# Attention and MLP kernel on one core: when weights and V are queued, over which queues the first loads go, and whether k or q is prepared first

## The chip, the cores and the metric

The kernel runs on one core of a Trainium2 chip. The time is device microseconds of that core. Three executions of the kernel before took 317.15, 321.90 and 322.06 us. A run is called "slow" when it is over 1.5% above the fastest of the same kernel, and "fast" otherwise.

A "span" is the length of one profiled execution from its first to its last instruction; it is some 2 us shorter than the time. The engines are TensorE (PE, weight loads PEld), VectorE (DVE), ScalarE (ACT), GpSimd (POOL) and SyncE (SP).

## The reference

Four batches, eight heads, 768 positions, 64 columns per head. Each query attends to the three best of twelve key blocks (by the mean key of the block) and to its own block, causally; then a token-mixing and a channel-mixing MLP run on the result.

```
k_rep = k.reshape(B, H, 12, 64, D).mean(axis=3)
gate  = einsum('bhsd,bhnd->bhsn', q, k_rep)          # causal blocks only
mask  = top 3 blocks of gate, and the own block; causal
x     = softmax(q k^T / 8, masked) v                  # heads side by side: (4, 768, 512)
u     = x + (relu(x^T w_tok1) w_tok2)^T
out   = u + relu(u w_ch1) w_ch2
```

## The kernel before

Two heads make a "pair"; there are 16 pairs, four to a batch. Each pair is prepared in four stages, all of them on chains that cross engines:

- `trq`: six float32 transposes of q on TensorE, a copy to SBUF on ScalarE, two casts on GpSimd.
- `trk`: the same for k, and on VectorE the block sums of k, put into `ks2`.
- `gate`: twelve small float32 matmuls (24 columns each) of q with `ks2`; top 3 on VectorE; result in `bn16`.
- `mask`: six transposes of `bn16`, two copies into the rows that extend q.

Then come scores, exponential (ScalarE), diagonal mask (VectorE) and the product with V (`av`). In the views below `tq` and `tk` are the transposes of q and k, `gps` the gate, `bps` the mask's transposes, `sps` the scores, `aps` the product with V; `qt`, `kt`, `kst` and `ks` are the copies of q and k, the block sums and `ks2`. The MLP work of a batch is strewn between the next batch's pairs, so pairs 0 to 3 have no MLP work beside them.

```python
    def load(i):                                   # q, k on SyncE's queue; V on GpSimd's (it casts to float16)
        ...
        for t, src in ((q32, q), (k32, k)):
            for g in range(2):
                nc.sync.dma_start(out=t[:, :, 64 * g:64 * g + 64], in_=src[b, h + g]...)
        for g in range(2):
            nc.gpsimd.dma_start(out=V16[r][:, g, :, 0:64], in_=v[b, h + g]...)
    ...
        def trk():
            ...
            nc.vector.tensor_reduce(out=kst, in_=kt.rearrange("p (n w) -> p n w", w=64), axis=AX.X, op=ALU.add)
            nc.vector.tensor_copy(out=ks2[r][64:128, 0:NB], in_=kst[64:128, :])
            nc.vector.tensor_copy(out=ks2[r][0:64, NB:2 * NB], in_=kst[0:64, :])
            nc.gpsimd.tensor_copy(out=KA[r][0][0:64, :], in_=kt[0:64, :])
            nc.gpsimd.tensor_copy(out=KA[r][1][64:128, :], in_=kt[64:128, :])
    ...
    preps[0]["trq"](); preps[0]["trk"](); preps[0]["gate"]()
    preps[1]["trq"](); preps[0]["mask"](); preps[1]["trk"]()
    load(2)
    wth = weight_loads()                           # ten pieces of 384 KB, on GpSimd's queue
    for i in range(NP):
        ...
        order = [scores(i, 0, 0)] + stage("gate", i + 1)
        order += [last_av] if last_av else []
        order += [scores(i, 0, 1)] + stage("trq", i + 2) + [scores(i, 0, 2), scores(i, 1, 0)]
        order += stage("mask", i + 1) + [av(i, 0), scores(i, 1, 1)] + stage("trk", i + 2)
        if i + 3 < NP:
            order.append(lambda: load(i + 3))
        if i < 3:
            take, wth = wth[:4], wth[4:]           # weights: no wait in front of the first six
            order += take
        order.append(scores(i, 1, 2))
        last_av = av(i, 1)
```

The order in the program is not quite the order on an engine: a scheduler places the instructions. In the kernel before it put V of pair 0, six weight pieces and V of pair 1 at the head of GpSimd's stream.

The softmax here doesn't subtract the row's maximum and nothing guards it: scores larger than these inputs give would overflow.

Of the kernel before, what the change touches and what calls it, by code (L numbers as in the profile page):

```python
# [9 lines left out]
FP = mybir.dt.float32  # L10
F16 = mybir.dt.float16
AF = mybir.ActivationFunctionType
ALU = mybir.AluOpType
# [13 lines left out]
def kernel(  # L27
# [11 lines left out]
    nc = tc.nc  # L39
    B, H, S, D = q.shape  # L40
    NB = S // 64
# [12 lines left out]
    def const(name, a, dt, eng):  # L54
        t = sp.tile(list(a.shape), dt, tag=name, name=name)
        eng.dma_start(out=t, in_=nc.inline_tensor(a, name=name + "c").ap())
        return t
# [7 lines left out]
    pairs = [(b, h) for b in range(B) for h in range(0, H, 2)]  # L65
    NP = len(pairs)

    loads = {}

    def load(i):  # L70
        b, h = pairs[i]
        q32 = sp.tile([128, NJ, 128], FP, tag="q32", bufs=3, name=f"q32_{i}")
        k32 = sp.tile([128, NJ, 128], FP, tag="k32", bufs=3, name=f"k32_{i}")
        for t, src in ((q32, q), (k32, k)):
            for g in range(2):
                nc.sync.dma_start(out=t[:, :, 64 * g:64 * g + 64],
                                  in_=src[b, h + g].rearrange("(j p) d -> p j d", p=128))
        r = i % (R + 1)
        for g in range(2):
            nc.gpsimd.dma_start(out=V16[r][:, g, :, 0:64],  # L80
                                in_=v[b, h + g].rearrange("(j p) d -> p j d", p=128))
        loads[i] = (q32, k32)

    R = 3
    V16 = [sp.tile([128, 2, NJ, 65], F16, tag=f"V{r}", name=f"V{r}") for r in range(R + 1)]
# [2 lines left out]
    ks2 = [sp.tile([128, 2 * NB], FP, tag=f"ks{r}", name=f"ks{r}") for r in range(R)]  # L88
    bn16 = [sp.tile([128, NJ, 2, 64], F16, tag=f"bn{r}", name=f"bn{r}") for r in range(R)]

    load(0)
    ident32 = const("id32", np.eye(128, dtype=np.float32), FP, nc.scalar)
    for r in range(R):
        nc.vector.memset(ks2[r], 0.0)
        nc.vector.memset(bn16[r], 0.0)
        nc.vector.memset(QA[r][0][64:128, :], 0.0)
        nc.vector.memset(QA[r][1][0:64, :], 0.0)
    for r in range(R + 1):
        nc.vector.memset(V16[r][:, :, :, 64:65], 1.0)
    pidx = np.arange(128)  # L100
    nidx = np.arange(NB)
    jidx = np.arange(NJ)
# [9 lines left out]
    ind64 = np.zeros((64, S), np.float16)  # L112
    ind64[0:NB] = ind_np
    ind_dram = nc.inline_tensor(ind64, name="indc").ap()
    for r in range(R):
        for x in range(2):
            lo = 64 if x == 0 else 0
            nc.sync.dma_start(out=KA[r][x][lo:lo + 64, :], in_=ind_dram)
        if r == 0:
            load(1)  # L120

    w1_16 = sp.tile([128, NJ, DT], F16, tag="w1", name="w1")
    w2_16 = sp.tile([128, 2, S], F16, tag="w2", name="w2")
# [3 lines left out]
    def weight_loads():  # L127
        w1 = moe_w_tok1.rearrange("(j p) t -> p j t", p=128)
        w2 = moe_w_tok2.rearrange("(g p) s -> p g s", p=128)
        c1 = moe_w_ch1.rearrange("(c p) f -> p c f", p=128)  # L130
        c2 = moe_w_ch2.rearrange("(g p) c -> p g c", p=128)
        th = [lambda: nc.gpsimd.dma_start(out=w1_16, in_=w1), lambda: nc.gpsimd.dma_start(out=w2_16, in_=w2)]
        th += [lambda c=c: nc.gpsimd.dma_start(out=wc1_16[:, c, :], in_=c1[:, c, :]) for c in range(NCC)]
        th += [lambda f=f: nc.gpsimd.dma_start(out=wc2_16[:, f:f + 3, :], in_=c2[:, f:f + 3, :])
               for f in range(0, NFC, 3)]
        return th
# [3 lines left out]
    def prep(i):  # L140
        r = i % R
        st = {}

        def trq():
            q32 = loads[i][0]
            ps = big("tq")
            for j in range(NJ):
                nc.tensor.transpose(out=ps[:, 128 * j:128 * j + 128], in_=q32[:, j, :], identity=ident32)  # L148
            qt = sp.tile([128, S], FP, tag="qt", bufs=2, name=f"qt_{i}")
            nc.scalar.copy(out=qt, in_=ps[:, 0:S])  # L150
            st["qt"] = qt
            nc.gpsimd.tensor_copy(out=QA[r][0][0:64, :], in_=qt[0:64, :])
            nc.gpsimd.tensor_copy(out=QA[r][1][64:128, :], in_=qt[64:128, :])

        def trk():
            k32 = loads[i][1]
            ps = big("tk")
            for j in range(NJ):
                nc.tensor.transpose(out=ps[:, 128 * j:128 * j + 128], in_=k32[:, j, :], identity=ident32)  # L159
            kt = sp.tile([128, S], FP, tag="kt", bufs=2, name=f"kt_{i}")  # L160
            nc.scalar.copy(out=kt, in_=ps[:, 0:S])  # L161
            kst = sp.tile([128, NB], FP, tag="kst", bufs=2, name=f"kst_{i}")
            nc.vector.tensor_reduce(out=kst, in_=kt.rearrange("p (n w) -> p n w", w=64),
                                    axis=AX.X, op=ALU.add)
            nc.vector.tensor_copy(out=ks2[r][64:128, 0:NB], in_=kst[64:128, :])
            nc.vector.tensor_copy(out=ks2[r][0:64, NB:2 * NB], in_=kst[0:64, :])
            nc.gpsimd.tensor_copy(out=KA[r][0][0:64, :], in_=kt[0:64, :])
            nc.gpsimd.tensor_copy(out=KA[r][1][64:128, :], in_=kt[64:128, :])

        def gate():  # L170
            gps = bank([128, NJ, 2 * NB], "gps")
            for j in range(NJ):
                nc.tensor.matmul(out=gps[:, j, :], lhsT=st["qt"][:, 128 * j:128 * j + 128],  # L173
                                 rhs=ks2[r], start=True, stop=True)
            gm = sp.tile([128, NJ, 2 * NB], FP, tag="gm", bufs=2, name=f"gm_{i}")
            m8 = sp.tile([128, NJ, 2, 8], FP, tag="m8", bufs=2, name=f"m8_{i}")
            lt = sp.tile([128, NJ, 2 * NB], FP, tag="lt", bufs=2, name=f"lt_{i}")
            nc.vector.tensor_tensor(out=gm, in0=gps, in1=gbias, op=ALU.add)
            for j in range(NJ):
                for x in range(2):  # L180
                    nc.vector.max(out=m8[:, j, x, :], in_=gm[:, j, NB * x:NB * x + NB])
            nc.vector.tensor_tensor(
                out=lt.rearrange("p j (x n) -> p j x n", n=NB),
                in0=gm.rearrange("p j (x n) -> p j x n", n=NB),
                in1=m8[:, :, :, 2:3].broadcast_to([128, NJ, 2, NB]), op=ALU.is_lt)
            nc.vector.scalar_tensor_tensor(out=lt, in0=lt, scalar=MASKV, in1=own, op0=ALU.mult, op1=ALU.max)
            nc.vector.tensor_copy(out=bn16[r][:, :, :, 0:NB], in_=lt.rearrange("p j (x n) -> p j x n", n=NB))

        def mask():
            bps = bank([128, S], "bps", F16)  # L190
            for j in range(NJ):
                nc.tensor.transpose(out=bps[:, 128 * j:128 * j + 128],  # L192
                                    in_=bn16[r][:, j, :, :].rearrange("p x n -> p (x n)"), identity=ident16)
            nc.vector.tensor_copy(out=QA[r][0][64:64 + NB, :], in_=bps[64:64 + NB, :])  # L194
            nc.vector.tensor_copy(out=QA[r][1][0:NB, :], in_=bps[0:NB, :])

        return dict(trq=trq, trk=trk, gate=gate, mask=mask)

    E = {}

# [44 lines left out]
    def mlp(b):  # L245
# [65 lines left out]
        return th  # L311

    preps = [prep(i) for i in range(NP)]
    preps[0]["trq"]()
    preps[0]["trk"]()
    preps[0]["gate"]()
    preps[1]["trq"]()
    preps[0]["mask"]()
    preps[1]["trk"]()
    load(2)  # L320
    wth = weight_loads()
    pend = []
    last_av = None
    for i in range(NP):
        b, h = pairs[i]

        def stage(name, n):
            return [preps[n][name]] if n < NP else []

        order = [scores(i, 0, 0)] + stage("gate", i + 1)  # L330
        order += [last_av] if last_av else []
        first = len(order)
        order += [scores(i, 0, 1)] + stage("trq", i + 2) + [scores(i, 0, 2), scores(i, 1, 0)]
        order += stage("mask", i + 1) + [av(i, 0), scores(i, 1, 1)] + stage("trk", i + 2)
        if i + 3 < NP:
            order.append(lambda: load(i + 3))
        if i < 3:
            take, wth = wth[:4], wth[4:]
            order += take
        order.append(scores(i, 1, 2))  # L340
        last_av = av(i, 1)

        share = sum(c for c, _ in pend) / (4 - i % 4)
        done = 0.0
        for n, f in enumerate(order):
            f()
            want = share * (n + 1 - first) / (len(order) - first)
            while n >= first and pend and done + pend[0][0] / 2 <= want:
                c, g = pend.pop(0)
                g()  # L350
                done += c
        if i % 4 == 3:
            for _, g in pend:
                g()
            if i == NP - 1:
                last_av()
            pend = mlp(b)
# [32 lines left out]
```

## Time and profile before

| what | before |
|---|---|
| span of the profiled execution | 316.6 us |
| TensorE busy | 280.0 us (88%) |
| first score matmul | 28.76 us |
| one of the pairs 1 to 3, from first exponential to first exponential | 10.8, 10.6, 10.5 us |

The page divides the span into 40 slices. Each digit of the row PE is the busy share of TensorE in tenths, of PEclk the granted clock (the share of its full clock that TensorE is given), of DMA the busy share of the transfer engines. From the kernel before:

```profile
PE   1325888888999999999999999999999999899994
...
PEclk9999598778899999999999999999999999999999
...
DMA  9999999675444445646324444330000011100022
```

A slice is 7.9 us. In the first four TensorE has little to do while the transfer engines are full; in the next six it is 80% busy at a lowered clock; after that it is nearly full. So there are three stretches with three limits.

What TensorE waited for up to 42 us (the waits view, its four longest; total us, times, longest):

```profile
PE tq L148 <- DMA q_1_119<-in_q_dram: 6.2, 1, 6.2
PE tq L148 <- DMA q_0_83<-in_q_dram: 5.9, 1, 5.9
PE gps L173 <- DVE ks_77 L166: 3.0, 1, 3.0
PE tk L159 <- DMA k_0_84<-in_k_dram: 2.5, 1, 2.5
```

And the transfers issued up to 28 us (KB each, median us from issue to landing):

```profile
wc_133<-in_moe_w_ch_dram POOLq DMA_DIRECT2D x4, 384.0 KB, 13.6
...
w_131<-in_moe_w_tok_dram POOLq DMA_DIRECT2D x1, 384.0 KB, 8.4
w_132<-in_moe_w_tok_dram POOLq DMA_DIRECT2D x1, 384.0 KB, 10.0
q_1_119<-in_q_dram SPq DMA_DIRECT2D x2, 192.0 KB, 15.8
k_1_120<-in_k_dram SPq DMA_DIRECT2D x2, 192.0 KB, 18.1
```

q and k of pair 1 took 16 and 18 us to land, in the company of six weight pieces that nothing needs before 81 us. On TensorE (its timeline; start us, us, engine, line, operation, out<-in, count; in brackets the idle time before it) the gate of pair 0 comes early and the first scores late:

```profile
14.44 2.73 PE L173 MATMUL gps<-ks_77,qt_142 128*128 128x24 f32 x12 [2.96 <-DVE ks_77 L166]
...
28.76 1.69 PE L212 MATMUL sps<-Q_65,K_71 128*128 128x512 f16 x6
```

The chain of work that ended last shows both limits (start us, us, what):

```profile
8.39 18.29 DMA k_1_120<-in_k_dram
...
52.09 0.80 ACT kt_506 L161
52.91 0.95 DVE kst_508 L163
54.10 0.68 DVE ks_77 L165
...
55.02 1.52 PE gps L173 x12
```

One transfer is 18.3 us of the chain; and in each of the pairs 1 to 3 the copy of k, the block sums, `ks` and the gate follow each other. TensorE's waits between 42 and 82 us say the same:

```profile
PE gps L173 <- DVE ks_79 L166: 1.2, 2, 0.6
PE gps L173 <- DVE ks_78 L166: 0.6, 1, 0.6
PE gps L173 <- DVE ks_77 L166: 0.6, 1, 0.6
```

A wait on the list is short; the chain behind it (copy, sums, `ks`) is longer, because TensorE runs out of other work late. The last reading is the clock, microsecond by microsecond (the prediction says "second" and means this; stretch, us, then busy us and count of PE, PEld, DVE, ACT, POOL; granted clock; DMA share; GB/s):

```profile
54.00:55.00 1.00, 0.42 (x5) 0.18 (x4) 0.95 (x4) 1.00 (x2) 0.75 (x1) 1.00 1.14 206
...
56.00:57.00 1.00, 1.00 (x19) 1.00 (x19) 0.39 (x2) 0.00 (x0) 0.00 (x0) 0.95 0.74 150
57.00:58.00 1.00, 1.00 (x7) 0.94 (x6) 1.00 (x14) 0.00 (x0) 0.78 (x1) 0.50 0.22 36
```

Some 3.4 us at half clock follow in this place, and again at 47, 67 and 77 us. I call them half-clock windows. (The 5 in the row PEclk is a longer one in pair 0, from 33.0 to 39.8 us.)

### The profile page before, as it was taken

What the parts mean: (1) busy time and instruction counts of PE and PEld (TensorE: products, weight loads), DVE (VectorE), ACT (ScalarE), POOL (GpSimd) and SP (SyncE); (2) the same over time, 40 slices, a digit from 0 to 9 for tenths busy, and PEclk for the clock granted to TensorE, in tenths of its full rate; (3) what the DMA queues carried; (4) which work ended last, traced back from release to release, by engine and by line L of the source; (5) the groups of instructions that cost most, each with busy time, mean ns of one, the idle gap of its engine ahead of it and who ended that gap; (6) DMA issues with size and microseconds to landing.
All of it is one profiled execution on the core that took longest, in us unless ns stands there. A gap on an engine that the chain in (4) does not pass through costs nothing.

```text
span 316.6 us, 5878 instructions
## 1 busy us (share of the span) xinstructions
PE 280.0 (88%) x2272; PEld 182.0 (57%) x2272; DVE 181.9 (57%) x624; ACT 141.4 (45%) x185; POOL 86.6 (27%) x110
## 2 busy tenths in 40 slices
PE   1325888888999999999999999999999999899994
PEld 1324665667557675656676766566766655456541
DVE  4223478667496666565975657576865644373321
ACT  2104268556465573526556644354666443214200
POOL 7606565444233333333222324140222000000000
PEclk9999598778899999999999999999999999999999
DMA  9999999675444445646324444330000011100022
GB/s 162 213 191 220 195 215 213 100 104 87 65 62 64 62 64 95 131 100 127 52 36 59 70 90 90 81 79 2 0 2 1 2 66 69 65 2 0 0 101 99
DMA packets 83179, 27.23 MB, mean 86 GB/s; under 512 B 76112, under 2 KB 79568, under 8 KB 83152
## 3 DMA queue, kind: packets, MB, share of 16 engines
q1 hardware_dynamic: 54112, 19.47, 26.5%
q0 software_dynamic: 28320, 7.08, 22.6%
q10 hardware_dynamic: 720, 0.31, 0.4%
q8 instruction: 18, 0.29, 0.4%
q14 instruction: 9, 0.07, 0.1%
HBM read 27.64 MB, written 6.29 MB: 107 GB/s over the span
## 4 chain that ended last, share of the span: by engine, by line
PE 76%; DVE 8%; DMA 7%; ACT 5%; issue 1%; ACTq 0%; SPq 0%
PE sps L212 10%; PE gps L173 7%; PE aps L233 6%; DMA k_1_120<-in_k_dram 6%; PE tq L148 3%; PE ups L267 3%; PE tk L159 3%; PE bps L192 2%; DMA id_113<-id16c 2%; DVE u_3626 L269 1%; PE utps L276 1%; PE c_3376 L299 1%; PE c_3925 L299 1%; PE c_3584 L299 1%; PE c_3485 L299 1%
## 5 line engine op out<-in xcount | busy, mean ns | idle before, releaser
L286 PEld LDWEIGHTS <-wc_133 128*128 128x128 f16 x384 | 37.1, 98 | 26.2 <-issue 0.8
L80 POOL DMA_DIRECT2D V_61<-in_v_dram x8 | 6.8, 847 | 23.7 <-PE aps L233 13.2
L212 PE MATMUL sps<-Q_65,K_71 128*128 128x512 f16 (+3 forms) x48 | 11.6, 330 | 0.7 <-ACT e_12_0_2820 L217 0.5
L299 PEld LDWEIGHTS <-h_3_3628 128*128 128x128 f16 x72 | 7.0, 97 | 8.3
L80 POOL DMA_DIRECT2D V_62<-in_v_dram x8 | 6.6, 828 | 18.6 <-PE aps L233 9.2
L80 POOL DMA_DIRECT2D V_64<-in_v_dram x8 | 6.6, 824 | 18.4 <-PE aps L233 11.5
L212 PE MATMUL sps<-Q_66,K_72 128*128 128x512 f16 (+3 forms) x48 | 10.6, 333 | 0.9 <-ACT e_3_1_820 L217 0.5
L299 PEld LDWEIGHTS <-h_2_2826 128*128 128x128 f16 x72 | 6.9, 98 | 7.3
L299 PEld LDWEIGHTS <-h_0_920 128*128 128x128 f16 x72 | 7.0, 98 | 7.2
L299 PEld LDWEIGHTS <-h_1_1873 128*128 128x128 f16 x72 | 7.0, 98 | 7.2
L212 PE MATMUL sps<-Q_68,K_74 128*128 128x512 f16 (+3 forms) x40 | 9.4, 324 | 1.3 <-ACT e_1_1_496 L217 0.5
L80 POOL DMA_DIRECT2D V_63<-in_v_dram x8 | 6.6, 826 | 13.8 <-PE sps L212 7.3
L212 PE MATMUL sps<-Q_69,K_75 128*128 128x512 f16 (+3 forms) x40 | 9.1, 313 | 0.8 <-ACT e_8_0_1867 L217 0.5
L212 PE MATMUL sps<-Q_67,K_73 128*128 128x512 f16 (+3 forms) x40 | 9.4, 322 | 0.5 <-ACT kt_343 L161 0.3
L212 PE MATMUL sps<-Q_70,K_76 128*128 128x512 f16 (+3 forms) x40 | 8.8, 321 | 0.9 <-ACT e_2_1_659 L217 0.5
L194 DVE COPY Q_65<-bps 12x768 f16<-12x768 f16 x6 | 3.3, 555 | 9.5 <-PE bps L192 9.4
L258 PEld LDWEIGHTS <-w_131 128*128 128x128 f16 x48 | 4.6, 98 | 6.1 <-issue 1.0
L212 PEld LDWEIGHTS <-K_72 128*128 128x128 f16 x48 | 4.8, 106 | 4.7 <-issue 2.3
L267 PEld LDWEIGHTS <-w_132 128*128 128x128 f16 x48 | 4.3, 97 | 5.4 <-issue 1.9
L148 PE MATMUL tq<-id_91,q_1_119 128*128 128x128 f32 x6 | 1.5, 425 | 6.2 <-DMA q_1_119<-in_q_dram 6.2
L148 PE MATMUL tq<-id_91,q_0_83 128*128 128x128 f32 x6 | 1.5, 425 | 5.9 <-DMA q_0_83<-in_q_dram 5.9
L212 PEld LDWEIGHTS <-K_71 128*128 128x128 f16 x48 | 4.7, 105 | 3.5 <-issue 1.7
(1023 smaller groups left out, 863.7 us busy)
## 6 DMA issues: line engine op xcount, KB each, us to landing
out_dram<-ob SPq DMA_DIRECT2D x24, 256.0 KB, 2.0
wc_133<-in_moe_w_ch_dram POOLq DMA_DIRECT2D x4, 384.0 KB, 13.6
wc_134<-in_moe_w_ch_dram POOLq DMA_DIRECT2D x4, 384.0 KB, 7.9
V_61<-in_v_dram POOLq DMA_DIRECT2D x8, 96.0 KB, 4.1
V_62<-in_v_dram POOLq DMA_DIRECT2D x8, 96.0 KB, 3.6
V_63<-in_v_dram POOLq DMA_DIRECT2D x8, 96.0 KB, 3.9
V_64<-in_v_dram POOLq DMA_DIRECT2D x8, 96.0 KB, 4.0
q_0_83<-in_q_dram SPq DMA_DIRECT2D x2, 192.0 KB, 3.9
```

The source lines that it names most:

```text
L80: nc.gpsimd.dma_start(out=V16[r][:, g, :, 0:64], in_=v[b, h + g].rearrange("(j p) d -> p j d", p=128))
L148: nc.tensor.transpose(out=ps[:, 128 * j:128 * j + 128], in_=q32[:, j, :], identity=ident32)
L159: nc.tensor.transpose(out=ps[:, 128 * j:128 * j + 128], in_=k32[:, j, :], identity=ident32)
L173: nc.tensor.matmul(out=gps[:, j, :], lhsT=st["qt"][:, 128 * j:128 * j + 128], rhs=ks2[r], start=True, stop=True)
L192: nc.tensor.transpose(out=bps[:, 128 * j:128 * j + 128], in_=bn16[r][:, j, :, :].rearrange("p x n -> p (x n)"), identity=ident16)
L194: nc.vector.tensor_copy(out=QA[r][0][64:64 + NB, :], in_=bps[64:64 + NB, :])
L212: nc.tensor.matmul(out=ps[:, off + a:off + a + n], lhsT=KA[r][x][:, 128 * kk:128 * kk + 128], rhs=QA[r][x][:, q0 + a:q0 + a + n], start=Tr ...
L233: nc.tensor.matmul(out=aps[:, jq, :], lhsT=E[i, x, g][:, o:o + 128], rhs=V16[i % (R + 1)][:, x, kk, :], start=(kk == 0), stop=(kk == jq))
L258: nc.tensor.matmul(out=mp, lhsT=w1_16[:, j, 128 * t:128 * t + 128], rhs=xs[b][:, j, :], start=(j == 0), stop=(j == NJ - 1))
L267: nc.tensor.matmul(out=mp, lhsT=w2_16[:, t, 128 * j:128 * j + 128], rhs=st["h1"][:, t, :], start=(t == 0), stop=(t == 1))
L286: nc.tensor.matmul(out=mp, lhsT=wc1_16[:, cc, 128 * fc:128 * fc + 128], rhs=st["uT"][:, cc, a:e], start=(cc == 0), stop=(cc == NCC - 1))
L299: nc.tensor.matmul(out=mp, lhsT=st["h2"][:, fc, 128 * j:128 * j + 128], rhs=wc2_16[:, fc, :], start=(fc == 0), stop=(fc == NFC - 1))
```

## The change

Its intent: weights and V shall not be in the way of the first q and k, so each is queued behind a key cast on GpSimd; the loads of pair 0 go out on two queues; k goes ahead of q everywhere, so that the block sums are done long before the gate wants them; `ks2` is made by one multiply with a constant instead of two copies.

```diff
-        for t, src in ((q32, q), (k32, k)):
+        for t, src in ((k32, k), (q32, q)):
             for g in range(2):
-                nc.sync.dma_start(...)
+                eng = nc.scalar if i == 0 and g == 1 else nc.sync
+                eng.dma_start(...)
...                                            # V of a pair is now a function of its own, loadv(i)
-            nc.vector.tensor_copy(out=ks2[r][64:128, 0:NB], in_=kst[64:128, :])
-            nc.vector.tensor_copy(out=ks2[r][0:64, NB:2 * NB], in_=kst[0:64, :])
+            nc.vector.tensor_tensor(out=ks2[r].rearrange("d (x n) -> d x n", x=2), in0=sel,
+                                    in1=kst.unsqueeze(1).broadcast_to([128, 2, NB]), op=ALU.mult)
...
-            nc.gpsimd.tensor_copy(out=KA[r][1][64:128, :], in_=kt[64:128, :])
+            st["k"] = nc.gpsimd.tensor_copy(out=KA[r][1][64:128, :], in_=kt[64:128, :])
...
-    preps[0]["trq"]()
     preps[0]["trk"]()
+    preps[0]["trq"]()
     preps[0]["gate"]()
+    preps[1]["trk"]()
+    behind(preps[0]["st"]["k"], [lambda: loadv(0)])
     preps[1]["trq"]()
     preps[0]["mask"]()
-    preps[1]["trk"]()
-    load(2)
-    wth = weight_loads()
+    behind(preps[1]["st"]["k"], [lambda: loadv(1), lambda: loadv(2)])
...
-        order += [scores(i, 0, 1)] + stage("trq", i + 2) + [scores(i, 0, 2), scores(i, 1, 0)]
-        order += stage("mask", i + 1) + [av(i, 0), scores(i, 1, 1)] + stage("trk", i + 2)
+        order += [scores(i, 0, 1)] + stage("trk", i + 2) + [scores(i, 0, 2), scores(i, 1, 0)]
+        order += stage("mask", i + 1) + [av(i, 0), scores(i, 1, 1)] + stage("trq", i + 2)
         if i + 3 < NP:
-            order.append(lambda: load(i + 3))
-        if i < 3:
-            take, wth = wth[:4], wth[4:]
-            order += take
+            order.append(lambda: (load(i + 3), behind(preps[i + 2]["st"]["k"], [lambda: loadv(i + 3)])))
+        if i < 4:
+            order.append(lambda: (behind(preps[i + 2]["st"]["k"], wth[:3]), wth.__delitem__(slice(0, 3))))
```

Cut: the constants and the memsets of the start are put in another order, the loads of pairs 1 and 2 and the constant rows of `KA` come earlier, and `behind(ins, fs)` issues transfers after an instruction of the same engine without a new wait.

## The prediction

> **What bounds it.** Three stretches of the span of 316.6 us. From 80 us TensorE is the limit: 64.9 of 66.0 us busy in 80-146 (windows view). From 0 to 28.7 us it is busy only 9.2 us: the first score matmul starts at 28.76 (timeline). TensorE's waits up to 42 us: 6.2 us for q of pair 1, 5.9 for q of pair 0, 2.5 for k of pair 0, 1.9 for k of pair 1. The chain of waits has one piece of 18.3 us for k of pair 1. Pair 1's loads took 15.8 and 18.1 us from issue to landing, while the software queue (V of pairs 0 and 1 and six weight pieces, all issued by 10.6 us) shared the engines, which moved about 200 GB/s. The Trainium skill's "DMA: Bandwidth & Descriptors", section "Queues, rings and completion order", says that an engine takes turns between queues packet by packet, which fits.
> From 28.7 to 80 us (pairs 0-3, no MLP work to fill in) it is latency: a pair takes 10.6 us; the chain runs K copy 0.80, reduce 0.95, two ks copies 0.74 + 0.17, gate matmuls 1.52. Once per pair the granted clock falls to 0.5 for some 3 us (47-50, 57-60, 67-70, 77-80), each time after a second of thin work (0.42-0.55 busy) before the gate matmuls. The skill's "TensorE: Matmul & The Clock Gate", section "What's actually happening", describes this: half rate after an idle window.
>
> **What the change does.**
> 1. No weights and no V ahead of the first loads. Loads of pairs 0 and 1 are 1.5 MB; at the traced 200 GB/s plus some 2.5 us of latency, k0 lands near 5, q0 near 7, q1 near 11 us (before: 23.3). The gate of pair 0 starts near 12 instead of 14.4, its mask near 16.5 instead of 27; TensorE now does mask and pair 1's gate before the first scores: these start at 20 (17.5 to 22.5) instead of 28.76. The third score group of pair 0, at 36.98 before, should come near 23-24. Gain 12 to 14 us, all critical.
> 2. k before q: the reduce and ks chain (about 2 us) leaves the path to the gate, which then waits only for the Q copy (0.80). About 1 us for each of pairs 1-3, and 1 to 1.7 us more where a half-clock window disappears. Estimate 4 us.
> 3. ks by one multiply instead of two copies: hidden. From 80 us on nothing: TensorE is full.
> 4. Costs: weights (3.9 MB) now come over pairs 0-3, with 0.96 MB of q, k, V each: about 2 MB per 10 us, the traced limit, but needed only from pair 4 on. The ACT queue waits for a landing before its table load (about 2 us, hidden behind q1).
>
> **Time.** 17 us off a mean near 320.5: 303.5 us; 8 in 10: 297 to 310. Faster by over 2%: 0.96; within: 0.03; slower: 0.01.
>
> **Signs.** Step 1 right: first scores at 17.5-22.5; q1 landing within 12 us; no wait for a DMA over 2 us on TensorE after 12 us; the same length (about 236 us) from batch 0's first token mixing to the end. Step 2 right: no waits for ks on the gate in pairs 1-3, fewer half-clock windows, a pair under 10 us.
>
> **Wrong if** q, k loads are slow also alone (then the start gains under 8 us); V of pair 0, issued only after six casts, makes the first AV wait; GpSimd blocks on transfers and delays casts; weights come too late for the first MLP; or the clock gate falls more often.

## The result, and the profile after

The changed kernel took 298.21 us in the median of four runs (296.91 to 300.04) against 321.0 for the kernel before. Ratios here are the mean time of one kernel's fast runs over that of the other's fast runs of the same rounds, so not quite the ratio of the medians: 0.9331, with a 95% interval from 0.9223 to 0.944. That is 6.7% faster; the median lies 5.3 us below the 303.5 foretold, inside the range of 297 to 310.

The same rows of the page, for the changed kernel; a slice is now 7.4 us:

```profile
PE   2869878899999999999999999999999999899994
...
PEclk9999999999999999999999999999999999999999
...
DMA  9999999998452648462261636140000011000022
```

The first stretch has become short and no slice shows a lowered clock (for the start this row misleads, as the warm start below shows). TensorE's waits up to 42 us:

```profile
PE tk L170 <- DMA k_0_86<-in_k_dram: 5.7, 1, 5.7
PE bps L203 <- DVE bn_80 L198: 2.3, 1, 2.3
...
PE tq L159 <- DMA q_0_85<-in_q_dram: 0.4, 1, 0.4
PE tq L159 <- DMA q_1_114<-in_q_dram: 0.2, 1, 0.2
```

After the first landing (5.7 us) no wait for a transfer is longer than 0.4 us. The loads of pair 1 take a third, or less, of what they took (transfers issued up to 20 us):

```profile
k_1_115<-in_k_dram SPq DMA_DIRECT2D x2, 192.0 KB, 6.2
q_1_114<-in_q_dram SPq DMA_DIRECT2D x2, 192.0 KB, 3.4
```

TensorE's timeline between 11 and 21.5 us:

```profile
12.41 2.60 PE L184 MATMUL gps<-ks_77,qt_157 128*128 128x24 f32 x12
...
17.99 0.82 PE L203 MATMUL bps<-id_110,bn_80 128*128 128x128 f16 x6 [2.28 <-DVE bn_80 L198]
18.61 2.70 PE L184 MATMUL gps<-ks_78,qt_210 128*128 128x24 f32 x12
21.13 0.60 PE L223 MATMUL sps<-Q_65,K_71 128*128 128x512 f16 x1
```

The gate of pair 0 starts at 12.41, the gate of pair 1 is done before the first scores, and these start at 21.13 instead of 28.76. In the pairs that follow, TensorE no longer waits for `ks`. Between 30 and 58 us its longest wait in total is for the copy that frees the accumulator of `av`:

```profile
PE aps L244 <- DVE x_0_327 L252: 2.2, 4, 0.7
```

Where the 20.9 us of the span went is read from the start of the first exponential of each pair in the two traces (ScalarE's timeline):

| first exponential of | before | changed | gained so far | gained in this stretch |
|---|---|---|---|---|
| pair 0 | 29.8 | 22.2 | 7.6 | 7.6 |
| pair 1 | 42.8 | 30.6 | 12.2 | 4.6 |
| pair 4 | 74.7 | 57.9 | 16.8 | 4.6 |
| pair 5 | 91.4 | 72.2 | 19.2 | 2.4 |
| end of the span | 316.6 | 295.7 | 20.9 | 1.7 |

Each of the pairs 1 to 3 takes 9.1 us instead of 10.5 to 10.8. Pair 4, in which the first MLP work comes in, also became shorter; the windows view of these stretches, first before, then changed:

```profile
74.70:91.40 16.70, 15.31 (x128) 10.33 (x128) 10.71 (x38) 7.88 (x11) 5.44 (x8) 0.90 0.50 72
```

```profile
57.90:72.20 14.30, 13.55 (x131) 9.06 (x131) 10.95 (x39) 8.01 (x11) 5.19 (x7) 1.00 1.17 166
```

For about the same matmuls TensorE is busy 1.8 us less and idle 0.6 us less; the mean clock was 0.90 and is 1.00. Over the whole span the same 2272 matmuls took 280.0 us before and 272.4 after.

### The profile page after: what moved, and what is told of

Read it like the earlier page. It is cut to its first block, busy times and chain, and to the rows that moved or that the text cites. A ratio compares the mean times of both kernels' runs of the same rounds, so it can differ in the third digit from the quotient of the medians.

```text
span 295.7 us, 5867 instructions
## 1 busy us (share of the span) xinstructions
PE 272.4 (92%) x2272; PEld 177.9 (60%) x2272; DVE 178.9 (60%) x605; ACT 141.4 (48%) x185; POOL 86.7 (29%) x110
## 4 chain that ended last, share of the span: by engine, by line
PE 81%; DVE 9%; ACT 4%; DMA 3%; issue 1%; SPq 0%; ACTq 0%
PE sps L223 11%; PE gps L184 8%; PE aps L244 7%; PE ups L278 3%; PE tq L159 3%; DMA k_1_115<-in_k_dram 2%; PE bps L203 2%; PE tk L170 2%; DVE u_3609 L280 1%; PE utps L287 1%; DMA q_1_114<-in_q_dram 1%; PE c_3359 L310 1%; DVE x_0_327 L252 1%; PE c_3908 L310 1%; PE c_3567 L310 1%
## 5 line engine op out<-in xcount | busy, mean ns | idle before, releaser
L223 PE MATMUL sps<-Q_65,K_71 128*128 128x512 f16 (+3 forms) x48 | 11.7, 334 | 1.2 <-ACT e_3_0_748 L228 0.5
L223 PE MATMUL sps<-Q_66,K_72 128*128 128x512 f16 (+3 forms) x48 | 10.0, 314 | 0.6 <-ACT e_3_1_816 L228 0.5
L223 PE MATMUL sps<-Q_69,K_75 128*128 128x512 f16 (+3 forms) x40 | 9.1, 305 | 1.2 <-ACT e_8_0_1856 L228 0.5
L223 PE MATMUL sps<-Q_67,K_73 128*128 128x512 f16 (+3 forms) x40 | 8.9, 305 | 1.2 <-ACT e_4_0_907 L228 0.5
L223 PE MATMUL sps<-Q_70,K_76 128*128 128x512 f16 (+3 forms) x40 | 8.3, 305 | 0.7 <-ACT e_2_1_655 L228 0.5
L223 PE MATMUL sps<-Q_68,K_74 128*128 128x512 f16 (+3 forms) x40 | 8.3, 306 | 0.5 <-ACT e_1_1_494 L228 0.5
L170 PE MATMUL tk<-id_83,k_0_86 128*128 128x128 f32 x6 | 1.5, 426 | 5.7 <-DMA k_0_86<-in_k_dram 5.7
L247 DVE RECIPROCAL rc<-aps 128x6 f32<-128x6 f32 x32 | 5.7, 180 | 0.7 <-PE aps L244 0.7
L280 DVE TENSOR_TENSOR u_3609<-x_3_2908,ups 128x512 f16<-128x512 f16 x6 | 3.7, 683 | 3.9 <-PE ups L278 3.9
```

The lines of the kernel that those rows point to most:

```text
L170: nc.tensor.transpose(out=ps[:, 128 * j:128 * j + 128], in_=k32[:, j, :], identity=ident32)
L223: nc.tensor.matmul(out=ps[:, off + a:off + a + n], lhsT=KA[r][x][:, 128 * kk:128 * kk + 128], rhs=QA[r][x][:, q0 + a:q0 + a + n], start=Tr ...
L247: nc.vector.reciprocal(out=rc.rearrange("p n o -> p (n o)"), in_=aps[:, :, 64:65].rearrange("p n o -> p (n o)"))
L280: nc.vector.tensor_tensor(out=st["u"][:, j, :], in0=xs[b][:, j, :], in1=mp, op=ALU.add)
```

## The experiments

Twelve kernels ran. Theory A, from the prediction and the two traces: two parts that add up, the start (12 to 14 us) by taking the weights out of the way, and the loop order (the rest) by taking the block sums off the path to the gate, with the half-clock windows going as a by-product. Rivals: the start gained by the order of instructions and the split of the loads rather than by the deferral; the loop gained by the clock rather than by the order. The first four kernels ran together, then four, then three, then one; each had its own runs of the kernel before (medians 320.3, 319.51, 318.94 and 319.72).

### The loop order alone, on the kernel before

```diff
-        order += [scores(i, 0, 1)] + stage("trq", i + 2) + [scores(i, 0, 2), scores(i, 1, 0)]
-        order += stage("mask", i + 1) + [av(i, 0), scores(i, 1, 1)] + stage("trk", i + 2)
+        order += [scores(i, 0, 1)] + stage("trk", i + 2) + [scores(i, 0, 2), scores(i, 1, 0)]
+        order += stage("mask", i + 1) + [av(i, 0), scores(i, 1, 1)] + stage("trq", i + 2)
```

> The kernel before with one change: k is transposed early and q late in each step of the main loop; nothing at the start is touched. Theory A (two additive parts; the loop order alone gave about 7 us between the third score group of pair 0 and the first token mixing, 44.2 to 36.9 us): first scores stay at 28 to 30 us, pairs 1 to 3 take about 9.1 us each instead of 10.6, half-clock windows after 42 us go, time 312 to 315 us. Rival B (the shorter pairs come from the new start, through transfers that no longer collide, and not from the order of k and q): pairs stay above 10.2 us, time above 318 us.

Measured: 318.57 us, ratio 0.9955 (0.9879 to 1.0032): the same as before. Both forecasts fell short: the pairs 1 to 3 took 9.7, 11.0 and 9.7 us, so the order did shorten the first and the last of them; the middle one holds a half-clock window (56.4 to 59.8 us). Two more windows (76.9 to 83.7 us) fell into pair 4, which took 16.8. And pair 0 took 15.4 us instead of 13.0: its third score group stood on TensorE behind the mask transposes of pair 1, which waited 1.5 us for `bn16`, and the k transposes of pair 2, and began at 40.4 us instead of 36.98. So the parts do not simply add: on the old start the order is worth 1.7 us by the medians, which is not clear of noise.

### The new start with the old loop order

The reverse of the diff above, on the changed kernel.

> The changed kernel with the loop order of before (q early, k late); the new start stays. Theory A: first scores at 21 us as in the changed kernel, pairs 1 to 3 back near 10.5 us, half-clock windows back, time 304 to 307 us. Rival B: pairs stay near 9.1 us and the time within 1 us of the changed kernel, about 298 us.

Measured: 304.22 us (303.55 to 304.58), ratio 0.9513. First exponential at 21.5 us, pairs 1 to 3 at 10.3 to 10.4 us each. Theory A holds: on the new start the loop order is worth 304.2 - 298.2 = 6.0 us. Note that only one of the three pairs, the last, holds a half-clock window (54.0 to 57.5 us); the other two take 10.3 and 10.4 us at full clock. With q first, then, 10.4 us is the length of the chain, not of the clock.

### The weights back at the head

On the changed kernel:

```diff
     wth = weight_loads()
+    for f in wth[:6]:
+        f()
+    wth = wth[6:]
+    loadv(0)
     preps[0]["trk"]()
...
-    behind(preps[0]["st"]["k"], [lambda: loadv(0)])
```

> The changed kernel with six weight pieces put back at the head of the software queue and V of pair 0 behind the first cast; order on TensorE unchanged. Theory A (contention between queues delayed q and k): q of pair 1 lands at 18 to 23 us instead of 11.6, first scores at 27 us or later, time 304 to 309 us. Rival C (the start gained by instruction order, k first, and the loads split over two queues): first scores within 3 us of 21, time below 301 us.

Measured: 317.68 us, ratio 0.995: with this one thing undone nearly all of the gain is gone, more than theory A said. The order of instructions on TensorE up to the first scores is the same as in the changed kernel. The chain of waits has two transfers in the place of the two short ones (start us, us, what):

```profile
1.81 15.64 DMA k<-in_k_dram
...
17.48 8.15 DMA q<-in_q_dram
```

The first scores start at 35.6 us, 14.5 later than in the changed kernel, and 6.9 later even than before. ScalarE's late table load (it stands at the issue of its last constant until q of pair 0 has landed, at 12.9 us) is not the reason: `ks` of pair 0 is there at 16.5 us. But in the new order the gate of pair 0 stands on TensorE behind transposes of k and q of pair 1, and so waits for their landing (timeline):

```profile
16.35 0.18 DVE L176 TENSOR_TENSOR ks<-sel,kst 128x24 f32<-128x24 f32 x1
...
22.64 1.51 PE L170 MATMUL tk<-id,k 128*128 128x128 f32 x6 [8.13 <-DMA q<-in_q_dram]
...
25.77 0.87 PE L159 MATMUL tq<-id,q 128*128 128x128 f32 x3 [1.61 <-DMA q<-in_q_dram]
...
26.43 2.59 PE L184 MATMUL gps<-ks,qt 128*128 128x24 f32 x12
```

In the kernel before the loads of pair 1 landed no earlier (TensorE could start on the last of them at 26.81), but the gate of pair 0 was at 14.44. By the first exponential of pair 1 the lag behind the kernel before is down to 2.3 us (45.1 against 42.8). So late loads cost more in the new order than in the old one, and the loss measured here is that of both together. That order and split alone made the start (rival C) is out. The Trainium skill's page "DMA: Bandwidth & Descriptors", section "Queues, rings and completion order", says that a transfer engine takes turns between the queues that have work for it. That fits what is seen: a transfer of 192 KB that lands in 3 to 6 us without the weights (pair 1 in the changed kernel) takes 16 to 18 with them (pair 1 in the kernel before).

### The deferral alone, on the kernel before

```diff
+    def loadv(i): ...                          # V apart from q and k, as in the change
...
+    behind(preps[0]["st"]["k"], [lambda: loadv(0)])
+    behind(preps[1]["st"]["k"], [lambda: loadv(1), lambda: loadv(2)])
...
-            order.append(lambda: load(i + 3))
-        if i < 3: ...
+            order.append(lambda: (load(i + 3), behind(preps[i + 2]["st"]["k"], [lambda: loadv(i + 3)])))
+        if i < 4:
+            order.append(lambda: (behind(preps[i + 2]["st"]["k"], wth[:3]), wth.__delitem__(slice(0, 3))))
```

> The kernel before with the deferral alone: V and weights queue behind the key casts, while the loads of pair 0 stay on one queue, q stays ahead of k everywhere, and the two ks copies stay. Theory A (deferral alone removes the contention, the rest of the start is small): q of pair 1 lands by 12 us, first scores near 19 to 22 us, time 304 to 308 us, within 3 us of the start-only kernel (304.2). Rival C (k first and the split queues carry a good part of the start): time above 309 us.

Measured: 309.61 us, ratio 0.9686 (0.9655 to 0.9717), just on the side of the rival in this forecast. The first exponential comes at 20.2 us, earlier than in the changed kernel, but pair 0 takes 12.9 us, as before, since the gate of pair 1 falls into it (at 22.84, after the first scores). So the deferral alone is worth about 10 us, not 14.

### The deferral, and k first at the start

```diff
-        for t, src in ((q32, q), (k32, k)):
+        for t, src in ((k32, k), (q32, q)):
...
-    preps[0]["trq"](); preps[0]["trk"](); preps[0]["gate"]()
-    preps[1]["trq"](); preps[0]["mask"](); preps[1]["trk"]()
+    preps[0]["trk"](); preps[0]["trq"](); preps[0]["gate"]()
+    preps[1]["trk"](); preps[1]["trq"](); preps[0]["mask"]()
```

> The deferral-only kernel (309.6 us) with k ahead of q in the loads and in the preparation of pairs 0 and 1, nothing else; loop order, one queue and the two ks copies stay. The start-only kernel, which also splits the loads, orders the constants anew and builds ks by one multiply, took 304.2. Theory D (the order of preparation carries those 5 us, because the gate of pair 1 then comes before the first scores and pair 0 is short): pair 0 takes 8 to 9 us instead of 13.0, time 303 to 306 us. Rival E (the split, the order of constants and the one multiply carry them): pair 0 stays above 11 us, time above 307 us.

The swap in `load` holds for all pairs, the other two for pairs 0 and 1. Measured: 306.74 us, ratio 0.9607 (0.9535 to 0.9679), between the two forecasts. Pair 0 takes 10.8 us instead of 12.9, with most of the gate of pair 1 (from 17.46) ahead of the first scores (19.59). The clock does not explain it, for TensorE ran at half rate through most of pair 0 in both: in the deferral-only kernel the record has it from 23.9 to 30.7 us, and here six transposes still took 1.49 us at 24.1 and 0.85 at 29.0. By the medians, the order of preparation is worth 309.6 - 306.7 = 2.9 us; the 2.5 us down to the start-only kernel belong to the split, the constants, the earlier loads of pairs 1 and 2, the one multiply and the scheduler's answer to them together, and I did not take those apart. The intervals of these kernels overlap, so the two parts are known to a microsecond or two.

### One queue for all loads of pair 0

```diff
-                eng = nc.scalar if i == 0 and g == 1 else nc.sync
+                eng = nc.sync
```

> The changed kernel with all loads of pair 0 on the one SyncE queue. If the split over two queues helps: 1 us or more slower than the changed kernel (298.2), k of pair 0 landing later. If it costs (ScalarE must wait for a landing before it may go on to its table load, 7.9 us in the changed kernel): the table load comes before 4.5 us, the first key copy near 8 instead of 9.2 us, time 296 to 298 us.

Measured: 297.81 us, ratio 0.9311 (0.9277 to 0.9345): the same as the changed kernel. The Trainium skill's page "DMA: Bandwidth & Descriptors", section "Issuing engines are not separate DMA queues", says that issuing on several engines saves only the sequencer's time. This run agrees: k of pair 0 let TensorE start at 5.13 us from one queue; from two it was 5.70 us in the changed kernel and 5.18 in the next one below. The split also has a price. ScalarE's table load, in the changed kernel and in this one (from their timelines):

```profile
7.87 1.28 ACT L172 ACT_TABLE_LOAD   x1 [7.87 <-DMA q_0_85<-in_q_dram]
```

```profile
3.57 1.28 ACT L172 ACT_TABLE_LOAD   x1 [3.57 <-DMA id<-id32c]
```

With two queues ScalarE has to wait for landings before it may issue its last constants (the last at 7.52 us, with one queue at 3.21), and the table load stands behind them. Here the first key copy came at 6.67 instead of 9.17 us and the third exponential of pair 0 at 24.5 instead of 25.6; a half-clock window in pair 1 (30.3 to 33.7 us, pair 1 10.5 us) took it back in this execution.

### The table load first

```diff
     load(0)
+    tiny = sp.tile([128, 1], FP, tag="tiny", name="tiny")
+    nc.vector.memset(tiny, 0.0)
+    nc.scalar.activation(out=tiny, in_=tiny, func=AF.Exp)
```

> The changed kernel plus a one-column exponential right behind the loads of pair 0, so that ScalarE loads its table before it waits for landings. Expected: table load done by 4 us, first key copy near 7.6 us instead of 9.17, gate of pair 0 1 to 2 us earlier where q of pair 1 lets it (it landed at 11.6), time 0.5 to 2 us below 298.2. Rival: q of pair 1 holds the same place on TensorE, so nothing changes.

Measured: 298.26 us, ratio 0.9327: nothing. The table was loaded by 3.6 us and the first key copy came at 8.00, but the gate of pair 0 started at 12.16 (12.41 in the changed kernel), behind the transposes of q of pair 1, and its VectorE work took the rest back. The rival is right. The prediction's "about 2 us, hidden behind q1" is thereby shown.

### Two copies for `ks` again

```diff
-            nc.vector.tensor_tensor(out=ks2[r]..., in0=sel, in1=kst..., op=ALU.mult)
+            nc.vector.tensor_copy(out=ks2[r][64:128, 0:NB], in_=kst[64:128, :])
+            nc.vector.tensor_copy(out=ks2[r][0:64, NB:2 * NB], in_=kst[0:64, :])
```

> The changed kernel with ks built by two copies again instead of one multiply with a mask tile. The prediction held it hidden: within 1 us of the changed kernel (298.2). Rival: the extra instruction on VectorE lies on the chain (VectorE stands in the chain of waits at 9% of the span): 1 us or more slower.

Cut: the constant `sel` goes, the memset of `ks2` comes back. Measured: 299.76 us (298.28 to 302.44), ratio 0.9393 with an interval from 0.9326 to 0.946, which overlaps that of the changed kernel. Its pairs 1 to 3 took 9.2 to 9.3 us instead of 9.1. This is inconclusive: hidden, or up to a microsecond and a half.

### Clock or order: filler matmuls

To tell the clock from the order, needless matmuls keep TensorE busy where it had little to do, on the start-only kernel and on the changed one:

```diff
-            gps = bank([128, NJ, 2 * NB], "gps")
+            gfull = bank([128, 512], "gps")
+            gps = gfull[:, 0:NJ * 2 * NB].rearrange("p (j n) -> p j n", n=2 * NB)
+            if 1 <= i <= 4:
+                for _ in range(8):
+                    nc.tensor.matmul(out=gfull[:, 0:256], lhsT=ident16, rhs=m0..., start=True, stop=True)
```

> The start-only kernel (q early, k late) with eight needless 128x128x256 matmuls ahead of the gate matmuls of pairs 1 to 4, into the same bank, which the gate then overwrites; the result is the same. The gate still waits for the ks chain. Clock theory: granted clock stays at 1.0 in pairs 1 to 3 and most of the loop's gain comes back, 299 to 303 us, 3 us or more below the start-only kernel. Wait theory (the ks chain itself costs the time, the clock little): within 1 us of the start-only kernel, or slower.

> The changed kernel with eight needless 128x128x256 matmuls ahead of the gates of pairs 1 to 4. With the start-only kernel, with and without the same fill (303.0 and 304.2), and the changed kernel (298.2) it makes a square: order of k and q, and half-clock windows. If the order alone carries the loop's gain: about 297 to 299 us, 4 to 6 us below the filled start-only kernel (303.0), with the clock at 1.0 in both. If the gain needed a warm clock and not the order, it would be within 2 us of 303.0.

Measured, medians in us:

| | no filler | filler (clock 0.994 to 1.0 in every run) |
|---|---|---|
| q early, k late, new start | 304.2 | 303.0 |
| k early, q late (the change) | 298.2 | 297.2 |

The order is worth 6.0 us without filler and 5.8 with it; the filler 1.2 and 1.0 us, which is within the noise of these intervals (0.9484 against 0.9513, 0.9312 against 0.9331). These gains are net: the filler has a price, for the first of it falls into pair 0, and the first exponential of pair 1 came 1.0 and 1.1 us later with it. The clock theory is out: with the filler the profiled execution of the start-only kernel has a recorded clock of 1.0 in all its pairs after pair 0, and its pairs 1 to 3 still take 10.2, 10.4 and 10.0 us; without filler, and so without its price, the two pairs at full clock took 10.3 and 10.4.

The clock is not without effect once the chain is short. With k first, those of the pairs 1 to 3 that held no window took 8.6 to 9.7 us, and those with one 10.0 to 11.1 (the loop-only, weights-at-head, one-queue, table-first and warm-start kernels). The four runs of the changed kernel say it too: 296.91 and 297.67 us at a mean clock of 1.0, 298.74 at 0.993, 300.04 at 0.986. From 297.3 (the mean of the first two) to 300.04 this is 2.7 us for 0.014 of the clock, two or three windows (a run with one had 0.993 or 0.994).

### A warm start

The gates of pairs 0 and 1 took 2.60 and 2.70 us in the changed kernel and 1.42 later (30.4 us). In the kernel before the first gate took 2.73. The page's clock row says full clock there, but these lengths say half. The row reads full wherever the trace holds no clock record, and the first record of the changed kernel's trace begins at 26.5 us. So, on the one-queue kernel:

```diff
+    wz = sp.tile([128, 512], F16, tag="wz", name="wz")
+    nc.gpsimd.memset(wz, 1.0)
+    def warm(n):
+        wp = bank([128, 512], "warm")
+        for _ in range(n):
+            nc.tensor.matmul(out=wp, lhsT=wz[:, 0:128], rhs=wz, start=True, stop=True)
+    warm(14)
     load(0)
...                                            # and warm(3), warm(4), warm(8) between the stages of pairs 0 and 1
```

> The no-split kernel plus 29 needless 128x128x512 matmuls on a constant tile during the start (14 before k of pair 0 lands, the rest in the gaps up to the mask of pair 0). Theory: TensorE runs at half rate until about 25 us in the changed kernel (gate of pair 0 and 1 took 2.60 and 2.70 us against 1.42 later), though the clock record says 1.0; kept busy from the start it is at full rate by 5 us, the two gates take 1.3 to 1.6 us each, first scores by 17 us instead of 20 to 21, time 293 to 295.5 us. Rival (the start is bound by landings and by VectorE's chain): first scores no earlier than 19 us, time 297 us or more.

Measured: 296.96 us (294.01 to 297.91), ratio 0.9287 (0.9238 to 0.9336). Its first scores come at 17.5 us and its first exponential at 18.1, but the time is longer than forecast, and the interval overlaps that of the one-queue kernel (0.9277 to 0.9345), so this gain is not clear of noise. In five of six runs the clock was below 0.99, with windows in the pairs, as at 26.8 to 30.2 us in the profiled one (pair 1 10.5 us).

The next kernel adds the filler, four matmuls to a gate:

> The same with four needless 128x128x256 matmuls ahead of the gates of pairs 1 to 4 as well, so that no half-clock window falls in the pairs. If such windows cost about 1.4 us each with k first (297.3 us without, 300.0 with two, in the changed kernel's own runs): clock 1.0 in every run, the spread of the times below 1.5 us, 0 to 1.5 us faster than the kernel with the warm start alone. Rival: the fill costs as much as it saves, equal or slower.

Measured: 293.30 us (292.44 to 294.12, and the slow run at 296.86), ratio 0.9173 (0.9132 to 0.9214). This is the fastest of all, 1.6% below the changed kernel by the medians; its interval touches neither that of the changed kernel nor that of the warm start alone. The forecast had less, 0 to 1.5 us against 3.7 by the medians, and a clock of 1.0 in every run, where one of the six had it and the fast ones had 0.993 or more. TensorE's timeline between 5 and 20 us:

```profile
10.71 1.49 PE L199 MATMUL gps<-ks,qt 128*128 128x24 f32 x12 [0.29 <-DVE ks L186]
...
16.16 0.51 PE L218 MATMUL bps<-id,bn 128*128 128x128 f16 x6 [1.21 <-DVE bn L213]
...
17.98 0.60 PE L238 MATMUL sps<-Q,K 128*128 128x512 f16 x3
```

The first gate takes 1.49 us instead of 2.60, the mask transposes 0.51 instead of 0.82, and the first scores come at 17.98 instead of 21.13. So up to the first scores TensorE ran at half rate in the kernel before and in the changed one, whatever the clock row says. The Trainium skill's page "TensorE: Matmul & The Clock Gate", section "What's actually happening", has this: half rate is the state at rest, and activity lifts it.

## Why the prediction was right or wrong

Point by point:

1. **Start, 12 to 14 us foretold.** Right. At the first exponential of pair 1 the gain was 12.2 us, as it was at the third score group of pair 0 (36.98 before, 24.73 now; foretold 23 to 24), the first scores came at 21.13 (foretold 17.5 to 22.5), q of pair 1 had landed by 11.75, and no wait for a transfer over 0.4 us followed. The cause is the deferral: undone alone, it cost 19.5 of 22 us, though in an order in which late loads cost more than before. What the prediction did not say is that the deferral by itself gives only 10 us; the order of preparation, which brings the gate of pair 1 ahead of the first scores, adds some 2.9, and the 2.5 beyond that were not taken apart.
2. **k before q, 4 us foretold in pairs 1 to 3.** The size was right, 4.6 us between the first exponentials of pair 1 and pair 4. Of its two terms one failed: "1 to 1.7 us more where a half-clock window disappears". At an unchanged full clock the order alone turned 10.4 us into 9.1, 1.3 us a pair where about 1 was foretold; taking the windows away with q first gave some 1 us over the whole kernel, net of the filler's price. So the sum came out near 4 partly by luck, one term larger and the other nearly absent. The order is the cause and the clock a lesser matter.
3. **"From 80 us on nothing: TensorE is full."** As the prediction's own sign counts it, from batch 0's first token mixing to the end, this nearly held: 235.6 us before, 234.2 now, 1.4 us where 0 was foretold. The term that was mis-sized is the one before it, for it stopped at pair 3. From the first exponential of pair 4 to the end, the kernel before took 241.9 us, the start-only kernel 241.5, the changed one 237.8: 4.1 us, of which 2.7 lie between that exponential and the first token mixing (6.37 us before, 3.63 now). So it is the loop order again: in pair 4 the MLP work comes in only after the first scores, so the latency chain still rules up to there. By the filler runs about half of what pair 4 gained (2.4 us) is clock (16.6 us with q first, 15.5 with filler, 14.3 with k first). I had read the busy share from 80 us on and let pair 4, which begins at 74.7, count as full.
4. **`ks` by one multiply, hidden.** Not settled (at most 1.5 us).
5. **Costs.** Right: no wait of TensorE for a weight or for V up to 80 us is on the list that I read, although the transfer engines are full for 66 us (nine slices) instead of 55 (seven). The late table load was hidden, as the table-first kernel shows.
6. **"Each time after a second of thin work".** The changed kernel contradicts it as a rule. It has longer thin stretches, of two microseconds, and kept its clock (windows view):

```profile
46.00:47.00 1.00, 0.55 (x6) 0.37 (x5) 0.94 (x3) 1.00 (x2) 1.00 (x2) 1.00 1.11 211
47.00:48.00 1.00, 0.49 (x4) 0.23 (x3) 0.97 (x4) 1.00 (x2) 1.00 (x3) 1.00 1.06 203
48.00:49.00 1.00, 1.00 (x13) 0.79 (x11) 0.33 (x2) 0.36 (x2) 0.95 (x2) 1.00 1.14 241
```

Filler takes the windows away, so idleness has a part in them; which idleness it takes stays open.

The total came out as 20.9 us in the traces where 17 were foretold: 12.2 for the start (13 in the middle of its range), 4.6 for pairs 1 to 3 (4 foretold), 2.7 for pair 4 up to the first token mixing (not in the forecast) and 1.4 for the rest (0 foretold).

## What to carry to other kernels

Look at what the queues carry before the first tile lands: transfers that are needed late and issued early share the engines with the ones that are needed first, and in this case no order of instructions on the engines made up for that (with the weights at the head, 317.7 us in the new order against 320.3 in the old). When a stage is bound by latency, ask which of its inputs has the longer tail behind it (here k, with sums and `ks`) and start that one first; expect the gain wherever the chain still rules, also at the edge of a stretch that looks full. A change can need another one to pay: the loop order was worth 6 us on the new start and 1.7 us, not clear of noise, on the old.

## What the Trainium skill lacked or had wrong

- "TensorE: Matmul & The Clock Gate", section "Seeing it yourself", warns that the recorded clock events are unreliable. It does not say that the clock before the first event may be half, which the profile views here, having no record, print as 1.00: in the changed kernel it is 1.00 in every slice and the first record begins at 26.5 us, while the first two gates took 2.60 and 2.70 us against 1.42 later, and 1.49 when TensorE was kept busy from 1.3 us on.
- The same page, section "What's actually happening", tells of a window that must be idle before the clock is halved, but not up to what busy share it counts as idle. In the kernel before the clock was halved at 57 us though TensorE had been 42% busy or more in each of the ten microseconds ahead of it, and in the changed kernel it was not halved after two at 55% and 49%.
- "DMA: Bandwidth & Descriptors", section "Queues, rings and completion order", says that queues take turns, without a size for what that costs. Here a load of 192 KB took 15.8 to 18.1 us from issue to landing beside six weight pieces of 384 KB, and 3.4 to 6.2 us without them.
- "DMA: Bandwidth & Descriptors", section "Issuing engines are not separate DMA queues", speaks of the time that an issue takes, not of constants issued on ScalarE's queue that hold up its compute: its table load came at 7.87 us when it had issued two of the first loads too, and at 3.57 us when it had not.
